# Decoding float64 weights in a routed-expert kernel: the weights' low halves made on VectorE, and the mantissa tail merged with the sign

## The chip, the cores and the metric

The kernel runs on one core of a Trainium2 chip. The metric is the device time of one launch in microseconds (us), the median of several runs. A profiled execution of the same program gives the trace; its own time is given beside its span below.

The engines are named as in the profile: PE (TensorE, the matrix multiplier), DVE (VectorE), ACT (ScalarE), POOL (GpSimd) and SP (which issues most of the loads).

## The reference

Three stages, one after the other, on 2304 tokens (4 batches of 576) of width 512:

```python
# 1. masked attention, 8 heads of 64; heads 0-3 see a local band of 32, heads 4-7 every 32nd position
scores = q @ k.T / 8;  attn = softmax(where(mask, scores, -1e9));  x = attn @ v
# 2. MLP with a PReLU, 512 -> 2048 -> 512, weights given as float64
h = x @ w_in;  g = maximum(h, 0) + alpha * minimum(h, 0);  x = g @ w_out
# 3. one of 8 experts for each token (argmax of x @ w_gate), 512 -> 1024 -> 512
y[t] = gate[t] * sigmoid(...)[t] * (relu(x[t] @ w1[e]) @ w2[e])
```

Only stage 1 and the first sixth of stage 2 matter here: that is where the float64 weights are turned into a form that PE can multiply.

## The kernel before

**The work and its order.** The MLP is cut into 6 blocks of 384 tokens and 16 chunks of 128 hidden columns; `n` counts the 96 pairs of block and chunk. For each `n`, `mlp_in` makes a 128x384 tile of h with 12 matmuls (lines 439 to 441), `mlp_act` applies the PReLU (ACT, lines 448 and 449; DVE, line 450), `mlp_split` splits the result into a high part `gh` (ACT, line 459) and a low part `gl` (DVE, line 460), and `mlp_out` adds it to three accumulators with 9 matmuls (lines 473 to 475). Three products of high and low parts stand in for one fp32 product. The loop runs two ahead: iteration `n` multiplies the weights of `n + 2` into h and the result of `n` into the accumulators.

Attention is cut into 48 steps. The first ten and their tails fill a prologue of 13 steps (about 6 to 47 us); the others are spread over the MLP loop, one in nearly each iteration of block 0. A step has its scores (PE), their maximum (DVE, line 252), the exponentials (ACT, line 281), the sums' reciprocals (DVE, lines 295 and 296), the normalisation (POOL, line 297), transposes (PE, line 313; ACT, line 315), the product with the values (PE, line 328) and its split into `xh` (ACT, line 367) and `xl` (DVE, line 372). The order on every engine is the order in which the code is written; each engine works its own list from the top.

**The decoding of a chunk.** A chunk's weights come as 128x1024 float64, loaded by SP into `raw` (in the code `raw64`), 8 KB for each partition. Each float64 is two 32-bit words, the low one first. Five instructions and a sixth turn them into fp32 and then into a high and a low part:

- `decode_a` (line 402, ACT): the upper word, read as a float and scaled, into a `stage` tile;
- `decode_b` (line 406, DVE): the stage tile shifted left by 3, which makes room for 3 more bits; (line 407, DVE): the low word shifted right by 29, ORed into it;
- `decode_s` (line 413, DVE): the sign of the upper word, ORed into it;
- `decode_c` (line 421, ACT): the high half of `w`, a rounded copy; (line 422, POOL): the low half, the difference.

The 16 chunks are decoded once, in the prologue (chunks 0 to 4) and in the first iterations of block 0 (5 to 15), and all 6 blocks use them. In iteration `n` the loop issues `decode_c` of chunk `n + 4`, `decode_b` and `decode_s` of chunk `n + 5`, and `decode_a` of chunk `n + 6`. `stage` has three buffers. The main loop, cut to what matters:

```python
if n + 2 < last: mlp_in(n + 2)
...                                     # values of an attention step
if n + 2 < last: mlp_act(n + 2)
if n + DEC < NC1: decode(n + DEC, 4)
...                                     # scores and maximum of a step
if n + DEC + 1 < NC1: decode(n + DEC + 1, 3)
mlp_out(n, range(1))                    # transposes, then the rest of mlp_out
if n + DEC + 2 < NC1: decode(n + DEC + 2, 1)
if n + 2 < last: mlp_split(n + 2)
```

Here `DEC` is 4, `NC1` is 16, and `decode(k, m)` issues those of the first `m` decoding steps of chunk `k` that were not issued before.

Of the kernel before, what the change touches and what calls it, by code (L numbers as in the profile page):

```python
# [7 lines left out]
F32 = mybir.dt.float32  # L8
F32R = mybir.dt.float32r
BF16 = mybir.dt.bfloat16  # L10
I32 = mybir.dt.int32
AF = mybir.ActivationFunctionType
ALU = mybir.AluOpType
X = mybir.AxisListType.X
# [9 lines left out]
NC1 = FF // P  # L24
# [18 lines left out]
DEC = 4  # L43
# [19 lines left out]
RS = 7  # L63
NEG = -1.0e9
BIG = 12582912.0
SIGN = -(2**31)

C_ID = 0
C_I8 = C_ID + P
# [14 lines left out]
def attention_prelu_mlp_routed_experts_kernel(  # L84
# [11 lines left out]
    nc = tc.nc  # L96
# [28 lines left out]
    with tc.manual_schedule():  # L125
# [144 lines left out]
        def att_exp(gi):  # L270
# [6 lines left out]
            if b < PE_MASK:  # L277
                nc.scalar.activation(out=nm[:r, : 2 * nj], in_=nm[:r, : 2 * nj], func=AF.Copy, scale=SCALE)
            for u in range(2 * nj):
# [3 lines left out]
                    in_=src,  # L283
                    func=AF.Exp,
                    bias=nm[:r, u : u + 1],
# [18 lines left out]
        def att_transpose(gi, tag):  # L304
# [9 lines left out]
            ptt = apool.tile([P, 4, P], F32, tag="pt", name="ptt", bufs=NPT_BUFS)  # L314
            nc.scalar.activation(out=ptt[:kk, :nu, :r], in_=tr[:kk, :nu, :r], func=AF.Copy)
            pt_t[gi] = ptt
# [20 lines left out]
        def att_store(gi):  # L337
# [28 lines left out]
            for src, dh, dl in moves:  # L366
                nc.scalar.activation(out=dh, in_=src, func=AF.Copy)
            px_t[gi] = moves
# [8 lines left out]
        raw_t, w_t = {}, {}  # L377

        def stage():
            return xpool.tile([P, 2 * (DM + 1)], F32, tag="stage", name="stage", bufs=3)  # L380
# [8 lines left out]
        def load_w(c):  # L389
            raw_t[c] = w_tile(c, I32, "raw64")  # L390
            nc.sync.dma_start(raw_t[c], wp[c].bitcast(I32))


        dec_t = {}

        def words(c):
            two = raw_t[c].rearrange("p (n two) -> p n two", two=2)
            return two[:, :, 0], two[:, :, 1]

        def decode_a(c):  # L400
            t = dec_t[c] = stage()[:, :1024]
            nc.scalar.activation(out=t, in_=words(c)[1].bitcast(F32), func=AF.Copy, scale=2.0**-112)

        def decode_b(c):
            t = dec_t[c].bitcast(I32)
            nc.vector.tensor_scalar(out=t, in0=t, scalar1=3, scalar2=None, op0=ALU.logical_shift_left)
            nc.vector.scalar_tensor_tensor(
                out=t, in0=words(c)[0], scalar=29, in1=t, op0=ALU.logical_shift_right, op1=ALU.bitwise_or
            )

        def decode_s(c):
            t = dec_t[c].bitcast(I32)
            nc.vector.scalar_tensor_tensor(
                out=t, in0=words(c)[1], scalar=SIGN, in1=t, op0=ALU.bitwise_and, op1=ALU.bitwise_or
            )
            raw_t.pop(c)

        def decode_c(c):
            t = dec_t.pop(c)
            w = w_t[c] = w_tile(c, F32R, "w")  # L420
            nc.scalar.activation(out=w[:, :1024], in_=t, func=AF.Copy)
            nc.gpsimd.tensor_tensor(out=w[:, 1024:], in0=t, in1=w[:, :1024].bitcast(F32), op=ALU.subtract)

        def w_in(c, part, k):
            return w_t[c][:, part * 1024 + k * P : part * 1024 + (k + 1) * P]
# [29 lines left out]
        def mlp_split(n):  # L455
            v = h_t.pop(n)
            gh = xpool.tile([P, BLK], F32R, tag="gh", name="gh", bufs=3)
            gl = xpool.tile([P, BLK], F32R, tag="gl", name="gl", bufs=2)
            nc.scalar.activation(out=gh, in_=v, func=AF.Copy)  # L459
            nc.vector.tensor_tensor(out=gl, in0=v, in1=gh.bitcast(F32), op=ALU.subtract)  # L460
            g_t[n] = (gh, gl)
# [606 lines left out]
        def load_ws(k):  # L1068
            for _, c in zip(range(k), loads):
                load_w(c)  # L1070
# [49 lines left out]
        steps_done = {}  # L1120

        def decode(k, n):

            steps = [decode_a, decode_b, decode_s, decode_c]
            for f in steps[steps_done.get(k, 0) : n]:
                f(k)
            steps_done[k] = max(steps_done.get(k, 0), min(n, 4))

        for s in range(NPRO):
            att_step(s, ("h", "h") if s % 2 else ("S", "X"), "acc0" if s % 2 else "T", "acc1" if s % 2 else "acc2")  # L1130
# [4 lines left out]
            if s == 4:  # L1135
# [3 lines left out]
                    out=wg_hl[:, :, 2 * E :], in0=wg_sb, in1=wg_hl[:, :, : 2 * E].bitcast(F32), op=ALU.subtract  # L1139
                )  # L1140
                nc.vector.memset(acc_oh[:, 0, :], 0.0)
            for k in range(NC1):
                n = s - (T0[k] if k < len(T0) else 99)
                if n >= 0:
                    decode(k, n + 1)

        span[:] = [FIRST + EXTRA if EXTRA < LV else 0, NG]
        decode(DEC, 3)
        decode(DEC + 1, 1)
        for n in range(2):  # L1150
            mlp_in(n, range(KD - 1, KD))
            mlp_act(n)
            mlp_split(n)
        last = NBLK * NC1
        turn_at, logits_at = {}, {}
        for blk in range(NBLK - 1):
            for j in range(TPB):
                c = 2 * j + 1 if blk < NBLK - 2 else j
# [11 lines left out]
        for n in range(last):  # L1170
            blk, c = divmod(n, NC1)
            todo = []
            if blk + 1 < len(steps_of) and c < NC1 - 2:
                s0, s1 = steps_of[blk + 1]
                k = s1 - s0
# [38 lines left out]
                rank(blk - 1)  # L1214
            mlp_out(n, range(2, TPB))
            load_ws(1)
            if n + DEC + 2 < NC1:
                decode(n + DEC + 2, 1)
            if n + 2 < last:
                mlp_split(n + 2)  # L1220
            if c == NC1 - 1 and blk == 3:
                s_a.close()
                epool = s_x.enter_context(tc.tile_pool(name="epool", bufs=1))
                idx_in = epool.tile([P, NSLOT], I32, name="idx_in")
                idx_out = epool.tile([P, NSLOT], I32, name="idx_out")
                idx_any = epool.tile([1, 1], I32, name="idx_any")
# [265 lines left out]
```

## Time and profile before

| what | value |
|---|---|
| median of 3 runs | 828.43 us (828.38 to 828.44) |
| the profiled execution | 827.54 us |
| its span, first to last instruction | 825.8 us |
| PE busy | 783.3 us (95% of the span) |
| DVE busy | 465.1 us (56%) |
| ACT busy | 427.6 us (52%) |
| POOL busy | 223.9 us (27%) |
| mean granted clock of PE | 0.978 |

The profiled execution is 0.89 us under the median and 1.74 us over its own span. A granted clock of 1.00 is 2.4 GHz, and 0.50 would be 1.2 GHz throughout.

How rows read. A timeline row has its start in us from the span's start, its length in us, the engine, the line of the code, the operation, output<-inputs, shapes, a count, and in brackets the idle time before it with what ended that. A row of a table of windows has the stretch, its length, the busy us of PE, PE's weight loads, DVE, ACT and POOL (with counts of instructions), the granted clock of PE, the share of the DMA engines and GB/s. A row of a group has its count, busy us, mean ns, and the idle time before it. A row of one line has minimum, median and maximum in ns.

### The profile page before, as it was taken

What the parts mean: (1) busy time and instruction counts of PE and PEld (TensorE: products, weight loads), DVE (VectorE), ACT (ScalarE), POOL (GpSimd) and SP (SyncE); (2) the same over time, 40 slices, a digit from 0 to 9 for tenths busy, and PEclk for the clock granted to TensorE, in tenths of its full rate; (3) what the DMA queues carried; (4) which work ended last, traced back from release to release, by engine and by line L of the source; (5) the groups of instructions that cost most, each with busy time, mean ns of one, the idle gap of its engine ahead of it and who ended that gap; (6) DMA issues with size and microseconds to landing.
All of it is one profiled execution on the core that took longest, in us unless ns stands there. A gap on an engine that the chain in (4) does not pass through costs nothing. (4 is left out here: it accounts for less than half of the span.)

```text
span 825.8 us, 13693 instructions
## 1 busy us (share of the span) xinstructions
PE 783.3 (95%) x5035; PEld 659.0 (80%) x5035; DVE 465.1 (56%) x980; ACT 427.6 (52%) x1057; POOL 223.9 (27%) x152
## 2 busy tenths in 40 slices
PE   7778889999999999999999999999989998999996
PEld 4566767888888888888898898889879876878884
DVE  4979997345544454556333434657695447854422
ACT  6847676445544454555333333265534656655542
POOL 2734444011100011111000000113474465546422
PEclk9789899999999999999999999999999999999998
DMA  9707411111200121101000100553224577787421
GB/s 342 303 1 298 167 56 49 33 33 46 84 18 1 47 87 64 36 11 39 2 1 1 39 1 1 204 191 125 56 90 159 176 268 250 281 290 270 161 88 41
DMA packets 22621, 91.04 MB, mean 110 GB/s; under 512 B 3082, under 2 KB 7312, under 8 KB 15376
## 3 DMA queue, kind: packets, MB, share of 16 engines
q1 hardware_dynamic: 18816, 78.52, 26.8%
q0 software_dynamic: 3728, 11.55, 4.0%
q8 instruction: 41, 0.67, 0.3%
q14 instruction: 36, 0.29, 0.1%
HBM read 105.78 MB, written 9.97 MB: 140 GB/s over the span
## 5 line engine op out<-in xcount | busy, mean ns | idle before, releaser
L439 PE MATMUL h<-xh,w 128*128 128x384 f32 x384 | 131.2, 342 | 4.1 <-DVE gl L460 3.8
L440 PE MATMUL h<-xl,w 128*128 128x384 f32 x384 | 130.5, 340 | 0.7 <-DVE xl L372 0.7
L441 PE MATMUL h<-xh,w 128*128 128x384 f32 x384 | 130.4, 340 | 0.0
L450 DVE SCALAR_TENSOR_TENSOR h<-h,nalpha,a 128x384 f32<-128x384 f32 x96 | 59.9, 624 | 116.1 <-ACT h L449 116.0
L473 PE MATMUL acc<-w,gh 128*128 128x512 f32 x288 | 125.3, 435 | 0.0
L297 POOL TENSOR_TENSOR p<-p,sm 96x512 f32<-96x512 f32 (+2 forms) x47 | 48.2, 1026 | 283.6 <-DVE sm L296 260.5
L888 DVE TENSOR_TENSOR wx<-raw,wx 128x1024 fp32r<-128x1024 f32 x72 | 97.1, 1392 | 46.9 <-ACT wx L886 46.6
L475 PE MATMUL acc<-w,gl 128*128 128x512 f32 x288 | 114.3, 397 | 0.0
L474 PE MATMUL acc<-w,gh 128*128 128x512 f32 x288 | 114.1, 396 | 0.0
L448 ACT ACTIVATE a<-h 128x384 f32<-128x384 f32 x96 | 47.2, 491 | 105.9 <-PE h L441 105.9
L886 ACT ACTIVATE wx<-raw 128x1024 fp32r<-128x1024 f32 x96 | 94.6, 1056 | 7.6 <-DMA raw<-in_wexp_dram 7.6
L1042 PE MATMUL acc<-wx,hh 128*128 128x512 f32 x304 | 97.0, 401 | 0.0
L888 POOL TENSOR_TENSOR wx<-raw,wx 128x1024 fp32r<-128x1024 f32 x24 | 63.1, 2629 | 90.7 <-ACT wx L886 90.6
L439 PEld LDWEIGHTS h<-xh,w 128*128 128x128 f32 x384 | 73.4, 191 | 9.6 <-DVE gl L460 5.5
L440 PEld LDWEIGHTS h<-xl,w 128*128 128x128 f32 x384 | 73.2, 191 | 4.8 <-DVE xl L372 1.0
L441 PEld LDWEIGHTS h<-xh,w 128*128 128x128 f32 x384 | 73.2, 191 | 0.0
L460 DVE TENSOR_TENSOR gl<-h,gh 128x384 fp32r<-128x384 f32 x96 | 53.3, 555 | 33.0 <-PE acc L475 18.2
L895 POOL DMA_INDIRECT xg<-rows,idx_in x23 | 29.3, 1274 | 145.4 <-ACT h L449 139.0
L1042 PEld LDWEIGHTS acc<-wx,hh 128*128 128x128 f32 x304 | 56.6, 191 | 11.2
L475 PEld LDWEIGHTS acc<-w,gl 128*128 128x128 f32 x288 | 54.6, 190 | 13.2
L459 ACT ACTIVATE gh<-h 128x384 fp32r<-128x384 f32 x96 | 46.7, 486 | 34.8 <-DVE h L450 34.7
L473 PEld LDWEIGHTS acc<-w,gh 128*128 128x128 f32 x288 | 54.5, 189 | 10.6 <-issue 0.3
(259 smaller groups left out, 1548.3 us busy)
## 6 DMA issues: line engine op xcount, KB each, us to landing
raw<-in_wexp_dram SPq DMA_DIRECT2D x64, 1024.0 KB
raw<-in_wp_dram SPq DMA_DIRECT2D x16, 1024.0 KB
qk<-in_qkv_dram SPq DMA_DIRECT2D x10, 576.0 KB
rows<-stage SPq DMA_DIRECT2D x15, 256.5 KB
v<-in_qkv_dram SPq DMA_DIRECT2D x8, 320.0 KB
qk<-in_qkv_dram SPq DMA_DIRECT2D x4, 384.0 KB
v<-in_qkv_dram SPq DMA_DIRECT2D x6, 256.0 KB
qk<-in_qkv_dram SPq DMA_DIRECT2D x4, 224.0 KB
```

Source lines behind the costliest of these rows:

```text
L297: (nc.vector if gi in NRV else nc.gpsimd).tensor_tensor(out=pt[:r, :nu, :kk], in0=pt[:r, :nu, :kk], in1=sm[:r, :nu].unsqueeze(2).to_broadc ...
L439: mm(ph[:, :BLK], w_in(c, 0, k), xh[:, k, :], start=(k == 0), stop=False)
L440: mm(ph[:, :BLK], w_in(c, 0, k), xl[:, k, :], start=False, stop=False)
L441: mm(ph[:, :BLK], w_in(c, 1, k), xh[:, k, :], start=False, stop=(k == KD - 1))
L450: nc.vector.scalar_tensor_tensor(out=v, in0=v, scalar=nalpha[:, c : c + 1], in1=a, op0=ALU.mult, op1=ALU.add)
L460: nc.vector.tensor_tensor(out=gl, in0=v, in1=gh.bitcast(F32), op=ALU.subtract)
L473: mm(o, gh[:, t], w_out(c, 0), start=(c == 0), stop=False)
L474: mm(o, gh[:, t], w_out(c, 1), start=False, stop=False)
L475: mm(o, gl[:, t], w_out(c, 0), start=False, stop=(c == NC1 - 1))
L886: nc.scalar.activation(out=w[:, :1024], in_=raw, func=AF.Copy)
L888: eng.tensor_tensor(out=w[:, 1024:], in0=raw, in1=w[:, :1024].bitcast(F32), op=ALU.subtract)
L1042: mm(po[i], h[:, h0 : h0 + P], wk[:, w0 : w0 + 512], start=st, stop=sp)
```

## The change

Two things are altered in the decoding. First, the 3 bits that the low word gives (its top 3) are no longer ORed in by an instruction of their own. A shift on 16-bit quarters (line 410 of the changed code) takes quarter 1 of each float64, shifts it right by 13 and writes it over quarter 2, the lower half of the upper word, in `raw` itself; `decode_a` has read that word before. The masked step of line 417 then takes the sign bit and those 3 bits out of the upper word together. Second, the low half of `w` is made by DVE (line 428) and not by POOL, in a step of its own, `decode_d`, which is issued later: behind `mlp_out` in the loop, one attention step later in the prologue. `decode(DEC + 1, 1)` moves from ahead of the first two `mlp_act` to behind them.

```diff
-SIGN = -(2**31)
+SIGN_AND_TAIL = -(2**31) + 7
...
         def decode_b(c):
             t = dec_t[c].bitcast(I32)
+            q = raw_t[c].bitcast(U16).rearrange("p (n four) -> p n four", four=4)
+            nc.vector.tensor_scalar(
+                out=q[:, :, 2], in0=q[:, :, 1], scalar1=13, scalar2=None, op0=ALU.logical_shift_right
+            )
             nc.vector.tensor_scalar(out=t, in0=t, scalar1=3, scalar2=None, op0=ALU.logical_shift_left)
-            nc.vector.scalar_tensor_tensor(
-                out=t, in0=words(c)[0], scalar=29, in1=t, op0=ALU.logical_shift_right, op1=ALU.bitwise_or
-            )
 
         def decode_s(c):
...
             nc.vector.scalar_tensor_tensor(
-                out=t, in0=words(c)[1], scalar=SIGN, in1=t, op0=ALU.bitwise_and, op1=ALU.bitwise_or
+                out=t, in0=words(c)[1], scalar=SIGN_AND_TAIL, in1=t, op0=ALU.bitwise_and, op1=ALU.bitwise_or
             )
...
         def decode_c(c):
-            t = dec_t.pop(c)
             w = w_t[c] = w_tile(c, F32R, "w")
-            nc.scalar.activation(out=w[:, :1024], in_=t, func=AF.Copy)
-            nc.gpsimd.tensor_tensor(out=w[:, 1024:], in0=t, in1=w[:, :1024].bitcast(F32), op=ALU.subtract)
+            nc.scalar.activation(out=w[:, :1024], in_=dec_t[c], func=AF.Copy)
+
+        def decode_d(c):
+            w = w_t[c]
+            nc.vector.tensor_tensor(
+                out=w[:, 1024:], in0=dec_t.pop(c), in1=w[:, :1024].bitcast(F32), op=ALU.subtract
+            )
...
-            steps = [decode_a, decode_b, decode_s, decode_c]
+            steps = [decode_a, decode_b, decode_s, decode_c, decode_d]
...
-        decode(DEC, 3)
-        decode(DEC + 1, 1)
         for n in range(2):
             mlp_in(n, range(KD - 1, KD))
             mlp_act(n)
             mlp_split(n)
+        decode(DEC, 3)
+        decode(DEC + 1, 1)
...
             mlp_out(n, range(2, TPB))
             load_ws(1)
+            if n + DEC < NC1:
+                decode(n + DEC, 5)
             if n + DEC + 2 < NC1:
                 decode(n + DEC + 2, 1)
```

DVE in one iteration of the loop (`n` = 1), before; the numbered `raw` is chunk 6:

```order
L450 SCALAR_TENSOR_TENSOR h<-h,nalpha,a 128x384
L252 TENSOR_REDUCE nm<-sl_bank 126x2
L252 TENSOR_REDUCE nm<-X 126x2
L406 TENSOR_SCALAR stage<-stage 128x1024
L407 SCALAR_TENSOR_TENSOR stage<-raw_533,stage 128x1024
L413 SCALAR_TENSOR_TENSOR stage<-raw_533,stage 128x1024
L460 TENSOR_TENSOR gl<-h,gh 128x384
```

and with the change:

```order
L458 SCALAR_TENSOR_TENSOR h<-h,nalpha,a 128x384
L253 TENSOR_REDUCE nm<-sl_bank 126x2
L253 TENSOR_REDUCE nm<-X 126x2
L410 TENSOR_SCALAR raw_532<-raw_532 128x1024
L413 TENSOR_SCALAR stage<-stage 128x1024
L417 SCALAR_TENSOR_TENSOR stage<-raw_532,stage 128x1024
L428 TENSOR_TENSOR w<-stage,w 128x1024
L468 TENSOR_TENSOR gl<-h,gh 128x384
```

The two-input step of line 407 is gone; the shift of quarters stands ahead of the other shift, and the subtraction for chunk 5 stands ahead of `gl`.

POOL in the same part of the loop, before:

```order
L297 TENSOR_TENSOR p<-p,sm 96x512
L422 TENSOR_TENSOR w<-stage,w 128x1024
L297 TENSOR_TENSOR p<-p,sm 126x4x126
L422 TENSOR_TENSOR w<-stage,w 128x1024
L297 TENSOR_TENSOR p<-p,sm 126x4x126
L422 TENSOR_TENSOR w<-stage,w 128x1024
```

and with the change:

```order
L298 TENSOR_TENSOR p<-p,sm 96x512
L298 TENSOR_TENSOR p<-p,sm 126x4x126 x2
L298 TENSOR_TENSOR p<-p,sm 72x2x72
L298 TENSOR_TENSOR p<-p,sm 96x512
L298 TENSOR_TENSOR p<-p,sm 126x4x126 x2
```

Only the normalisations are left on POOL in this stretch.

## Rows read from the trace of the kernel before

**Rows 1.** Table of windows: the prologue, the loop's parts, all that follows block 0.

```profile
14.30:49.30 35.00, 25.97 (x184) 16.99 (x180) 33.04 (x61) 25.85 (x91) 22.93 (x11) 0.85 0.64 254
49.30:62.53 13.23, 11.45 (x51) 10.25 (x52) 8.52 (x11) 6.22 (x12) 2.49 (x1) 0.75 0.05 13
62.53:136.59 74.06, 62.87 (x382) 49.03 (x380) 71.74 (x105) 52.60 (x154) 33.43 (x19) 0.95 0.42 151
136.59:148.69 12.10, 11.87 (x84) 9.79 (x85) 5.05 (x15) 7.32 (x29) 5.47 (x4) 1.00 0.13 38
154.15:590.00 435.85, 435.01 (x2676) 377.44 (x2675) 211.09 (x579) 201.01 (x568) 44.84 (x40) 1.00 0.15 51
```

**Rows 2.** Table of waits, DVE's own, 62.53 to 136.59: total us, times, longest.

```profile
DVE xl L372 <- ACT xh L367: 1.0, 1, 1.0
DVE h L450 <- ACT h L449: 0.3, 1, 0.3
```

**Rows 3.** Timeline of DVE, one iteration of the loop.

```profile
100.04 0.15 DVE L295 TENSOR_SCALAR sm<-sm 96x4 f32<-96x4 f32 x1
...
101.56 0.41 DVE L252 TENSOR_REDUCE nm<-X 126x2 f32<-126x252 f32 x1
101.88 2.65 DVE L406 TENSOR_SCALAR stage<-stage 128x1024 int32<-128x1024 int32 x1
104.57 1.22 DVE L407 SCALAR_TENSOR_TENSOR stage<-raw,stage 128x1024 int32<-128x1024 int32 x1
105.83 1.22 DVE L413 SCALAR_TENSOR_TENSOR stage<-raw,stage 128x1024 int32<-128x1024 int32 x1
```

**Rows 4.** Timeline of POOL in the same iteration.

```profile
100.57 1.04 POOL L297 TENSOR_TENSOR p<-p,sm 96x512 f32<-96x512 f32 x1 [3.98 <-DVE sm L296]
101.57 2.42 POOL L422 TENSOR_TENSOR w<-stage,w 128x1024 fp32r<-128x1024 f32 x1
```

**Rows 5.** Groups of DVE instructions, 62.53 to 136.59.

```profile
L406 DVE TENSOR_SCALAR stage<-stage 128x1024 int32<-128x1024 int32 x10 | 21.1, 2106 | 0.0
L407 DVE SCALAR_TENSOR_TENSOR stage<-raw,stage 128x1024 int32<-128x1024 int32 x10 | 18.4, 1845 | 0.3
```

**Rows 6.** Single lines over the whole span: minimum, median and maximum in ns.

```profile
L406 DVE TENSOR_SCALAR stage<-stage x16: 675/804/2997, 14.3 to 130.6; 128x1024 int32<-128x1024 int32 x16
...
L888 DVE TENSOR_TENSOR wx<-raw,wx x72: 1210/1220/3426, 543.8 to 807.6; 128x1024 fp32r<-128x1024 f32 x72
...
L422 POOL TENSOR_TENSOR w<-stage,w x16: 2355/2498/3350, 23.0 to 137.6; 128x1024 fp32r<-128x1024 f32 x16
```

**Rows 7.** Timeline of DVE: the PReLU step that marks an iteration.

```profile
62.53 0.62 DVE L450 SCALAR_TENSOR_TENSOR h<-h,nalpha,a 128x384 f32<-128x384 f32 x1
...
136.59 0.62 DVE L450 SCALAR_TENSOR_TENSOR h<-h,nalpha,a 128x384 f32<-128x384 f32 x1
...
148.69 0.62 DVE L450 SCALAR_TENSOR_TENSOR h<-h,nalpha,a 128x384 f32<-128x384 f32 x1 [0.41 <-ACT h L449]
```

**Rows 8.** Timeline of DVE, prologue and the loop's first iteration.

```profile
24.28 2.05 DVE L295 TENSOR_SCALAR sm<-sm 126x4 f32<-126x4 f32 x1
...
32.87 0.81 DVE L295 TENSOR_SCALAR sm<-sm 126x4 f32<-126x4 f32 x1 [0.78 <-ACT p L281]
...
39.43 2.33 DVE L295 TENSOR_SCALAR sm<-sm 72x2 f32<-72x2 f32 x1
...
46.20 3.18 DVE L413 SCALAR_TENSOR_TENSOR stage<-raw,stage 128x1024 int32<-128x1024 int32 x1
49.30 0.61 DVE L450 SCALAR_TENSOR_TENSOR h<-h,nalpha,a 128x384 f32<-128x384 f32 x1
...
57.55 3.34 DVE L407 SCALAR_TENSOR_TENSOR stage<-raw,stage 128x1024 int32<-128x1024 int32 x1
```

**Rows 9.** Timelines of ACT and PE around the end of the prologue.

```profile
47.30 0.49 ACT L449 ACTIVATE h<-h 128x384 f32<-128x384 f32 x1
...
51.08 0.69 PE L439 MATMUL h<-xh,w 128*128 128x384 f32 x1 [3.69 <-DVE gl L460]
```

More of the change, by code (lines that the diff above doesn't have):

```diff
@@ L11 @@
 I32 = mybir.dt.int32
+U16 = mybir.dt.uint16
 AF = mybir.ActivationFunctionType
@@ L1122, in decode @@
         def decode(k, n):
-            steps = [decode_a, decode_b, decode_s, decode_c]
+            steps = [decode_a, decode_b, decode_s, decode_c, decode_d]
             for f in steps[steps_done.get(k, 0) : n]:
                 f(k)
-            steps_done[k] = max(steps_done.get(k, 0), min(n, 4))
+            steps_done[k] = max(steps_done.get(k, 0), min(n, 5))
         for s in range(NPRO):
```

## Prediction, made before the changed kernel ran

> **What bounds the kernel now.** I read the table of windows first. From 154.15 us on PE is busy 435.01 of 435.85 us while DVE has half of its time free [rows 1]: whatever comes before that only moves the rest forward or back, us for us. Before it the order is the other way round. In the ten loop iterations from 62.53 to 136.59 us DVE is busy 71.74 of 74.06 us and PE only 62.87, at a granted clock of 0.95 (1.00 is 2.4 GHz); in the prologue, 14.30 to 49.30 us, DVE is busy 33.04 of 35.00 us, PE 25.97 [rows 1]. In those ten iterations DVE's own waits come to 1.3 us together [rows 2], so the others wait for DVE. An iteration takes (136.59 - 62.53) / 10 = 7.41 us; the two behind them, with attention but with no decoding left on DVE, take 12.10 / 2 = 6.05 us, and there PE is full and at 1.00 [rows 1, 7]. So 6.05 us is what PE needs, and DVE costs 1.36 us more in each iteration.
>
> The timeline of one iteration says why. Line 406 takes 2.65 us there, and the 128x1024 steps behind it 1.22 us each [rows 3]; line 406 alone takes 0.68 us [rows 6]. While it is stuck, POOL makes a low half, 101.57 to 103.99 us [rows 4], and line 406 ends 0.54 us after that. In the next case it is line 407 that is stuck, for 3.34 us [rows 8]. One of the two is held in every iteration: over the ten their means are 2.11 and 1.85 us instead of 0.68 and 1.22 [rows 5], which is (2.11 - 0.68) + (1.85 - 1.22) = 2.06 us of an iteration. POOL's subtraction costs DVE about what one on DVE would cost, and more.
>
> **The change, part by part.**
>
> *A, the ten iterations.* Removed from DVE: the 2.06 us of being held, and line 407 itself, 1.22 us [rows 3]. Added: the subtraction and the shift of quarters. The subtraction has a row of its own kind, 128x1024 fp32r from two fp32 tiles: 1.21 us undisturbed [rows 6]. The shift is not in the trace: 1024 two-byte elements, 8 bytes apart, in and out. From below it is bounded by line 406, also a one-input shift of 1024 elements, 0.68 us [rows 6]; I see no reason for less, since the elements are not dense. From above it is bounded by line 407, which reads one input 8 bytes apart at 1.22 us and is no slower than line 413 or the dense subtraction [rows 3, 6], so the step in itself costs a reader nothing. I take 0.68 us, the row of the same operation. One more instruction adds one gap, 0.04 us (104.57 - 101.88 - 2.65) [rows 3]. DVE's iteration becomes 7.41 - 2.06 - 1.22 + 0.68 + 1.21 + 0.04 = 6.06 us. PE's need is 6.05 us. Two engines that are equally full and wait for each other do not both run without gaps; I take 6.2 us. Gain: 74.06 - 62.0 = 12.1 us.
>
> The Trainium skill, VectorE: DVE Perf Modes, in "What auto-detection actually checks", lets an instruction with one source and both sides in SBUF run two results a cycle, and asks for a step of one element only for packing two-byte values. By that rule the shift costs what line 406 does; were it to fall to one result a cycle, the row of line 407 would be its price and the time would be that of the first rival below.
>
> *B, the iteration before them* (from 56.30 to 62.53 us, without attention). Line 407 is held there, 3.34 us [rows 8]. The change removes 3.34 and adds 0.68 + 1.21 + 0.04: 1.4 us less on DVE. The clock in that window is 0.75 [rows 1], so PE is near; I take 1.0 us.
>
> *C, the prologue.* POOL's four subtractions hold three tiny steps (line 295: 2.05, 0.81 and 2.33 us, where 0.15 is normal [rows 3]) and the last masked step (3.18 instead of 1.22 us) [rows 8]: 1.90 + 0.66 + 2.18 + 1.96 = 6.7 us. Five steps of line 407 become shifts, 5 x 0.54 = 2.7 us less. Four subtractions come in, 4 x 1.21 = 4.8 us more. Sum 4.6 us less on an engine that is busy 94% of that stretch [rows 1]. That is the upper end, because ACT and PE have chains of their own there. The lower end is the last hold alone: ACT ends line 449 at 47.79 us, and line 450 starts only at 49.30 [rows 8, 9], 1.5 us later, and PE then waits 3.69 us for the `gl` behind it [rows 9]. I take the middle, 3.0 us.
>
> *What moves at no cost.* `decode_a` of chunk 5 (ACT, 1.1 us) goes behind the first two PReLUs; PE's wait of 3.69 us [rows 9] covers it, and without that cover it would delay the third `gh` by its length once. The low half is now ready some 3 us later than POOL had it, but its chunk is multiplied two iterations on. The subtraction adds a wait of DVE for ACT's high half; ACT starts that right behind line 449, as DVE starts line 450, and five DVE steps lie between. Queued behind it on DVE is `gl`, for which PE waits. `raw` stays in use exactly as long as before, so SP's loads and every DMA keep their place. The `stage` buffer is freed one part of an iteration later, and ACT writes it again an iteration after that.
>
> *Sum.* 12.1 + 1.0 + 3.0 = 16.1 us off the profiled 827.54: 811.4 us. The median stands 0.89 us above that execution, so **812.3 us**.
>
> **The rivals.**
>
> *The shift runs at half the pace*, 1.22 us. For it: its elements are two bytes wide and apart, unlike line 406's. Against: line 406 is otherwise the same operation. DVE's iteration is then 6.60 us, with the same addition of 0.14 about 6.75; A gives 6.6, B 0.9 and C 2.0 us (5 x 0.54 = 2.7 us less on DVE there): 9.5 us, **818.9 us**.
>
> *POOL still holds DVE.* The normalisations stay on POOL (1.04 us), one in each iteration. Now they run from 100.57 to 101.61 us, while DVE does steps that are not held, and the first shift comes at 101.88 [rows 3, 4]: 0.27 us later. If that margin went, the shift would be held by up to 1.04 us in each of the ten iterations: 10.4 us of A are lost, **822.7 us**. Against: the five DVE steps between the reciprocal and the shift are the same ones, in the same order. The Trainium skill, SBUF — State Buffer, "Who interferes with whom", has DVE's two-input steps contend with any GpSimd instruction that reads SBUF, and one-input steps in a two-port mode shut it out and be shut out. That speaks against putting both new steps on DVE while POOL keeps a task; no run here shows it for a 2-byte shift.
>
> *Slower: the shift writes badly.* Every output is two bytes in the middle of a word and 8 bytes from the next; no row shows such a write. If it takes what POOL's pass over as many elements takes, 2.50 us [rows 6], DVE's iteration is 6.06 + 1.82 = 7.88 us: A loses 4.7 us, B 0.4 and C 4.5 (5 x 1.82 less 4.6), together 9.6 us, **838.0 us**. It decides against the change in the loop from a shift of 0.68 + 1.35 = 2.03 us. For it: nothing but the gap in the trace. Against: strided reads cost nothing here.
>
> *It does not do what it says:* the holds are not POOL's. Then the 2.06 us stay, and the iteration is 7.41 - 1.22 + 0.68 + 1.25 = 8.1 us, 7 us slower. Against: each of the holds in the loop ends within about a step's length of POOL's subtraction. This is the same side as the last one and counts with it.
>
> **How the numbers follow.** The forecast, a shift near 0.68 us and no new hold, has 0.66; the shift at half pace 0.17; POOL's normalisation holding DVE 0.07; the two slower ones 0.07 together; 0.03 for a gain that ACT or PE eat up wholly. About 0.2% (1.7 us) is what a measurement here can tell from no change. Low end: A at PE's 6.05 us gives 13.6, B 1.4, C 4.6, and the clock something besides: at 0.75 over 13.23 us [rows 1] about 3.3 us of full-speed work are lost, and half of that may come back if PE waits less, 1.7 us. Sum 21.3, so 807 us. High end: the half-pace rival with C at 1.5 and B at 0.5, 8.6 us, so 820 us. The range 807 to 820 leaves out POOL's hold and the slower cases. Faster 0.91, same 0.03, slower 0.06.
>
> **What would show it.** Right: the ten iterations measured from PReLU step to PReLU step at 6.1 to 6.3 us; line 413 of the changed code (the old shift) at 0.68 us and line 417 at 1.22 us with hardly any spread; the shift of quarters at about 0.68; the subtraction at 1.21; PE's granted clock up in 49 to 137 us; everything after block 0 as long as before. Wrong: a shift at 1.2 us or above; spread in lines 410, 413 or 428 that ends with a normalisation on POOL; DVE waiting for ACT ahead of line 428; or the loop at 6.2 us and the end not earlier, which would mean that time is given back behind 154 us.

## The result, and the profile after

The changed kernel takes **814.92 us** (median of four runs, 814.50 to 817.12), the kernel before 828.43 us beside it (four runs, 828.38 to 831.42): 13.5 us less, a ratio of 0.9834 with a 95% interval of 0.9805 to 0.9862. The forecast was 812.3 us, its range 807 to 820. The execution that was profiled is the longest of the four, 817.12 us; against the profiled 827.54 us of before it is 10.4 us shorter, and what separates 10.4 from 13.5 comes up below.

Lines of the changed kernel have moved: the reciprocal is line 297 and POOL's normalisation 298 (296 and 297 before), the shift of quarters is line 410, the old shift 413 (406), the masked step 417 (413), the subtraction, now on DVE, 428 (422), the PReLU step 458 (450). Line 407 is gone.

The profile's first part, of the changed kernel: span, then busy time, share and instructions of each engine.

```profile
span 815.3 us, 13671 instructions
...
PE 780.9 (96%) x5032; PEld 658.7 (81%) x5035; DVE 453.8 (56%) x996; ACT 427.6 (52%) x1057; POOL 182.8 (22%) x136
```

DVE has 16 instructions more and POOL 16 fewer, which are the subtractions. The table of windows follows, cut at the same PReLU steps as [rows 1]: prologue, the steps before the ten iterations, the ten iterations, the two behind them, and a long stretch of what follows block 0.

```profile
15.22:48.76 33.54, 25.00 (x182) 16.51 (x180) 31.36 (x66) 24.91 (x90) 12.12 (x7) 0.85 0.63 250
48.76:60.59 11.83, 10.05 (x48) 9.08 (x49) 7.50 (x12) 7.91 (x14) 0.00 (x0) 0.86 0.01 0
60.59:123.49 62.90, 59.65 (x386) 47.84 (x384) 62.21 (x115) 51.80 (x153) 8.09 (x9) 1.00 0.48 176
123.49:135.58 12.09, 11.86 (x84) 9.80 (x85) 6.10 (x16) 7.20 (x29) 3.11 (x3) 1.00 0.20 64
141.08:536.97 395.89, 395.05 (x2376) 339.80 (x2375) 186.75 (x531) 180.54 (x537) 30.73 (x31) 1.00 0.13 44
```

Ten iterations take 62.90 us instead of 74.06 [rows 1], 6.29 us each instead of 7.41. DVE is still the engine that is full in them: busy 62.21 of 62.90 us, and the table of its own waits is empty there, where it had 1.3 us [rows 2]. POOL's 33.43 busy us have shrunk to 8.09, the normalisations alone. PE's granted clock is 1.00 instead of 0.95. The last window ends with the last PReLU step; before, the stretch between the same two places took 395.88 us, so behind block 0 nothing was given back up to there.

The timeline of DVE, one iteration of the changed kernel, beside [rows 3]:

```profile
98.10 0.61 DVE L458 SCALAR_TENSOR_TENSOR h<-h,nalpha,a 128x384 f32<-128x384 f32 x1
98.62 0.41 DVE L253 TENSOR_REDUCE nm<-sl_bank 126x2 f32<-126x252 f32 x1
98.95 0.41 DVE L253 TENSOR_REDUCE nm<-X 126x2 f32<-126x252 f32 x1
99.28 1.36 DVE L410 TENSOR_SCALAR raw<-raw 128x1024 uint16<-128x1024 uint16 x1
100.41 0.76 DVE L413 TENSOR_SCALAR stage<-stage 128x1024 int32<-128x1024 int32 x1
101.20 1.23 DVE L417 SCALAR_TENSOR_TENSOR stage<-raw,stage 128x1024 int32<-128x1024 int32 x1
102.34 1.22 DVE L428 TENSOR_TENSOR w<-stage,w 128x1024 fp32r<-128x1024 f32 x1
103.47 0.55 DVE L468 TENSOR_TENSOR gl<-h,gh 128x384 fp32r<-128x384 f32 x1
```

and of POOL in it, beside [rows 4]:

```profile
98.15 1.03 POOL L298 TENSOR_TENSOR p<-p,sm 126x504 f32<-126x504 f32 x1 [5.45 <-DVE sm L297]
```

Three things stand here. The old shift, line 413, takes 0.76 us; it took 2.65 us in [rows 3]. POOL's normalisation ends at 99.18 us, 0.10 us ahead of the first long step of this iteration. And the shift of quarters takes 1.36 us, not 0.68. The groups of DVE's long steps in the ten iterations say the same of all of them, beside [rows 5]:

```profile
L410 DVE TENSOR_SCALAR raw<-raw 128x1024 uint16<-128x1024 uint16 x10 | 13.6, 1361 | 0.0
L417 DVE SCALAR_TENSOR_TENSOR stage<-raw,stage 128x1024 int32<-128x1024 int32 x10 | 12.3, 1225 | 0.3
L428 DVE TENSOR_TENSOR w<-stage,w 128x1024 fp32r<-128x1024 f32 x10 | 12.2, 1218 | 0.0
L413 DVE TENSOR_SCALAR stage<-stage 128x1024 int32<-128x1024 int32 x10 | 7.3, 731 | 0.0
```

The 0.10 us are not there in every iteration. In four of the ten the normalisation ends 0.12 to 0.24 us behind the start of the shift. In the two where that is most, the shift takes 1.44 and 1.45 us instead of 1.32 to 1.36. One of them, DVE's line and POOL's:

```profile
105.28 1.45 DVE L410 TENSOR_SCALAR raw<-raw 128x1024 uint16<-128x1024 uint16 x1
```

```profile
104.48 1.03 POOL L298 TENSOR_TENSOR p<-p,sm 126x504 f32<-126x504 f32 x1 [5.30 <-DVE sm L297]
```

**Where the time went.** Stretches between marks of the timelines, in us. The marks are DVE's first instruction of line 295 (296 now) and PReLU steps by number; the last column runs from the last PReLU step to the end of the span. "Changed again" is the same kernel in experiment 10 (below).

| | start to first mark | to 1st PReLU | to 4th | to 14th (ten iterations) | to 96th, the last | to the end |
|---|---|---|---|---|---|---|
| before | 8.40 | 40.90 | 13.23 | 74.06 | 413.44 | 275.77 |
| changed | 9.32 | 39.44 | 11.83 | 62.90 | 413.48 | 278.33 |
| changed again | 8.54 | 39.20 | 11.78 | 62.89 | 413.42 | 276.87 |

In the profiled execution the gain is 1.46 us in the prologue, 1.40 in the next stretch and 11.16 in the ten iterations. Of these 14.0 us, 0.92 are lost ahead of the first mark and 2.56 behind the last PReLU step, in the expert stage, where the instructions are the same. In experiment 10's execution of the same kernel those two losses are 0.14 and 1.10 us; in a third one, experiment 1, they are 0.91 and 2.51 us, near the first. So the second to fourth columns are the change; what stands ahead of them and behind block 0 differs between executions of one kernel.

### The profile page after: what moved, and what is told of

The parts are those of the page before. It is cut to its first block, busy times and chain, and to the rows that moved or that the text cites. A ratio compares the mean times of both kernels' runs of the same rounds, so it can differ in the third digit from the quotient of the medians.

```text
span 815.3 us, 13671 instructions
## 1 busy us (share of the span) xinstructions
PE 780.9 (96%) x5032; PEld 658.7 (81%) x5035; DVE 453.8 (56%) x996; ACT 427.6 (52%) x1057; POOL 182.8 (22%) x136
## 4 chain that ended last, share of the span: by engine, by line
PE 75%; DVE 9%; issue 3%; ACT 3%; POOL 0%; DMA 0%; SPq 0%; ACTq 0%; DVEq 0%; POOLq 0%
PE acc L1050 10%; PE acc L481 8%; PE acc L483 7%; PE h L447 7%; PE h L449 7%; PE acc L482 7%; PE h L448 7%; PE T L329 2%; PE sl_bank L235 2%; DVE wx L896 2%; PE T L314 1%; PE h L973 1%; PE h L975 1%; PE h L974 1%; PE sl_bank L914 1%
## 5 line engine op out<-in xcount | busy, mean ns | idle before, releaser
L298 POOL TENSOR_TENSOR p<-p,sm 96x512 f32<-96x512 f32 (+2 forms) x47 | 49.9, 1061 | 331.0 <-DVE sm L297 278.0
```

The source lines that it names most:

```text
L298: (nc.vector if gi in NRV else nc.gpsimd).tensor_tensor(out=pt[:r, :nu, :kk], in0=pt[:r, :nu, :kk], in1=sm[:r, :nu].unsqueeze(2).to_broadc ...
```

## The experiments

Each difference is against the changed kernel. On the three chips the kernel before had medians of 829.22 us (first four runs), 827.98 (next four) and 828.23 (last three); ratios are against the one on the same chip.

**1. The changed kernel as it is** (r1_same). No edit.

> The changed kernel again, unaltered. In its first profile the lead over the kernel before is 13.07 us from the end of block 0 to the end of the MLP, and 10.5 us at the end: 2.6 us are lost in the expert stage. Theory A (chance of that one execution, in the loads of the experts' weights): the new profile keeps a lead of about 13 us to its end, time 814.5 to 815.1 us. Theory B (the change itself costs time behind the MLP): the new profile loses 2 to 3 us in the expert stage again, time about 817 us. Ten loop iterations about 62.9 us by either.

Measured: 816.93 us (four runs), ratio 0.9853 (0.9820 to 0.9885); ten iterations 62.89 us; from the last PReLU step to the end 278.28 us. The loop repeats to 0.01 us, and the longer expert stage came back too, which by this run alone looked like a property of the new schedule. Experiments 2, 6 and 10 say more on that.

**2. The subtraction back on POOL** (r2_pool_sub), the merged shift kept.

```diff
         def decode_c(c):
...
+            nc.gpsimd.tensor_tensor(out=w[:, 1024:], in0=dec_t.pop(c), in1=w[:, :1024].bitcast(F32), op=ALU.subtract)
         def decode_d(c):
-            w = w_t[c]
-            nc.vector.tensor_tensor(
...
+            pass
```

> The changed kernel with one part undone: the subtraction of the low half is on POOL again, right behind ACT's high half; the shift of quarters and the merged mask stay. Theory A (the holds of DVE by POOL's subtraction are what the change removed, so that they come back): about 2 us of holding in each of ten iterations, iteration 7.2 to 7.4 us, the kernel at 826 to 828 us. Theory B (the new shift, one input and one result a cycle, is not held, so that POOL's pass runs beside it and only the rest of the pass holds the step behind): holding about 1 us, iteration 6.2 to 6.5 us, the kernel at 815 to 818 us, and the subtraction could have stayed on POOL.

Measured: 827.14 us (12 runs), ratio 0.9982 (0.9963 to 1.0000): nearly the whole gain is gone. The ten iterations take 73.14 us, 7.31 each. The groups of DVE's instructions in them:

```profile
L410 DVE TENSOR_SCALAR raw<-raw 128x1024 uint16<-128x1024 uint16 x10 | 23.2, 2321 | 0.0
...
L413 DVE TENSOR_SCALAR stage<-stage 128x1024 int32<-128x1024 int32 x10 | 15.7, 1570 | 0.0
L417 DVE SCALAR_TENSOR_TENSOR stage<-raw,stage 128x1024 int32<-128x1024 int32 x10 | 14.3, 1430 | 0.3
```

One iteration of the same kernel, DVE's timeline, and POOL's:

```profile
101.32 3.29 DVE L410 TENSOR_SCALAR raw<-raw 128x1024 uint16<-128x1024 uint16 x1
```

```profile
101.00 2.42 POOL L425 TENSOR_TENSOR w<-stage,w 128x1024 fp32r<-128x1024 f32 x1
```

The loop's long holds are back with POOL's subtraction: against the changed kernel the means of the three steps are up by 0.96, 0.84 and 0.20 us, 2.0 us of an iteration. POOL's step ends at 103.42 us and the shift 1.19 us later, somewhat less than its own length behind it. The 2-byte shift is held like the 4-byte one, though it runs at half the pace of that (experiments 5 and 9).

**3. The old way to put the quarter in** (r3_old_tail), the subtraction left on DVE.

```diff
-SIGN_AND_TAIL = -(2**31) + 7
+SIGN_AND_TAIL = -(2**31)
...
-            q = raw_t[c].bitcast(U16).rearrange("p (n four) -> p n four", four=4)
-            nc.vector.tensor_scalar(
-                out=q[:, :, 2], in0=q[:, :, 1], scalar1=13, scalar2=None, op0=ALU.logical_shift_right
-            )
...
+            nc.vector.scalar_tensor_tensor(
+                out=t, in0=words(c)[0], scalar=29, in1=t, op0=ALU.logical_shift_right, op1=ALU.bitwise_or
+            )
```

> The changed kernel with the other part undone: the low word is shifted and ORed in by a two-input step again, as before, and there is no shift of quarters; the subtraction stays on DVE. Theory A (removing POOL's pass from beside DVE is the main gain): no holds, iteration 2.31 + 0.71 + 1.26 + 1.15 + 1.14 = 6.6 us at most, the kernel at 816 to 819 us. Theory B (the gain came with the shift): iteration 7.2 us or more, the kernel at 825 us or above.

Measured: 817.17 us (four runs), ratio 0.9847 (0.9815 to 0.9878); ten iterations 63.72 us, 6.37 each. The groups:

```profile
L410 DVE SCALAR_TENSOR_TENSOR stage<-raw,stage 128x1024 int32<-128x1024 int32 x10 | 12.2, 1225 | 0.3
L416 DVE SCALAR_TENSOR_TENSOR stage<-raw,stage 128x1024 int32<-128x1024 int32 x10 | 12.2, 1224 | 0.3
L427 DVE TENSOR_TENSOR w<-stage,w 128x1024 fp32r<-128x1024 f32 x10 | 12.2, 1218 | 0.0
L409 DVE TENSOR_SCALAR stage<-stage 128x1024 int32<-128x1024 int32 x10 | 7.0, 700 | 0.0
```

So the whole gain of the loop but 0.8 us is the subtraction's move. The second half of the change, the merged step, is worth 63.72 - 62.90 = 0.8 us in the ten iterations, and in the medians nothing that these runs tell apart. The two halves add to within 0.2 us: in the profiled executions the last PReLU step comes at 550.03 us before, at 549.05 with the merged step alone (experiment 2), at 537.79 with the move alone and at 536.97 with both.

**4. No quarter at all** (r4_no_tail): as experiment 3, without the old step that is added there; the 3 lowest bits are left out.

> The changed kernel without the shift of quarters: the lowest 3 bits of the mantissa are left out and the mask takes the sign alone. DVE has 1.1 us less in each iteration. Theory A (DVE still sets the pace at 6.29 us): the iteration falls to what PE needs, 6.05 us or a little above, the kernel 2 to 3 us faster than the changed one, about 812.5 us. Theory B (PE and its waits already set 6.29 us): iteration 6.2 to 6.3 us, the kernel within 1 us of the changed one.

Measured: 811.75 us (five runs), ratio 0.9786 (0.9759 to 0.9813); ten iterations 60.33 us, 6.03 each. The window of them, and DVE's own waits there:

```profile
57.26:117.59 60.33, 59.31 (x387) 48.70 (x387) 52.26 (x104) 51.33 (x154) 8.53 (x10) 1.00 0.49 180
```

```profile
DVE h L454 <- ACT h L453: 2.9, 9, 0.5
DVE xl L373 <- ACT xh L368: 2.7, 6, 0.6
DVE sm L296 <- ACT p L282: 1.2, 2, 0.9
```

Now PE is full, 59.31 of 60.33 us, DVE has 8 us free and waits for ACT. That is the floor under the loop, 6.03 us an iteration. It also prices the shift: 0.26 us per iteration of the loop lies over that floor, half of the 5.2 us between the medians of experiments 1 and 4; 1.4 us more are gained in the prologue and 0.9 in the stretch behind it.

**5. What makes the shift slow** (r5_prices). The shift's line takes another form from chunk to chunk: another element size, another distance.

```diff
+            v = (0, 1, 2, 3, 0, 4, 1, 2, 3, 0, 4, 1, 2, 3, 0, 4)[c]
+            if v == 0:
                 ...
+            elif v == 1:
+                nc.vector.tensor_scalar(out=r32[:, :, 0], in0=r32[:, :, 0], scalar1=29, ...)
+            elif v == 2:
+                nc.vector.tensor_scalar(out=r16[:, :1024], in0=r16[:, :1024], scalar1=0, ...)
+            elif v == 3:
+                nc.vector.tensor_scalar(out=t2[:, :, 0], in0=t2[:, :, 0], scalar1=0, ...)
+            else:
+                nc.vector.tensor_scalar(out=r8[:, :, 4], in0=r8[:, :, 3], scalar1=5, ...)
```

> The changed kernel with the shift in five forms, one form for each chunk, 1024 elements each, done in place; the 3 bits are left out in all of them and the mask takes the sign alone. Forms: 2-byte elements 8 bytes apart (as in the change); 4-byte elements 8 bytes apart; 2-byte elements side by side; 2-byte elements 4 bytes apart; single bytes 8 bytes apart. Read where POOL is idle. Theory A (the 8-byte step costs the pace): 4-byte elements 8 bytes apart take 1.2 to 1.3 us as well, 2-byte elements 4 bytes apart about 0.7 us. Theory B (2-byte elements that are not side by side cost it): 4-byte elements 8 bytes apart take 0.7 us, 2-byte elements 4 bytes apart 1.2 to 1.3 us. By both, 2-byte elements side by side take 0.4 to 0.7 us.

Measured, in DVE's timeline of the loop: line 415 is the form of the change, 419 whole 4-byte words that lie 8 bytes apart, 423 2-byte elements side by side, 428 2-byte elements 4 bytes apart, 432 single bytes 8 bytes apart. Each has 128x1024 elements.

```profile
76.88 1.34 DVE L415 TENSOR_SCALAR raw<-raw 128x1024 uint16<-128x1024 uint16 x1
...
83.38 1.33 DVE L432 TENSOR_SCALAR raw<-raw 128x1024 uint8<-128x1024 uint8 x1
...
89.86 0.69 DVE L419 TENSOR_SCALAR raw<-raw 128x1024 int32<-128x1024 int32 x1
...
95.59 0.41 DVE L423 TENSOR_SCALAR raw<-raw 128x1024 uint16<-128x1024 uint16 x1
...
101.22 0.77 DVE L428 TENSOR_SCALAR raw<-raw 128x1024 uint16<-128x1024 uint16 x1
```

Neither theory of this run fits. The distance of 8 bytes is not it (0.69 us with words), and 2-byte elements apart are not it either (0.77 us at 4 bytes). Among these forms only elements smaller than a word and 8 bytes apart fall to 1.33 us. That is what was seen, and not yet the rule: the forms that keep the pace lie one or two elements apart, the slow ones four or eight, so a rule by the step in elements fits as well. Words 16 bytes apart would tell the two from each other; they were not run.

**6. The kernel before once more** (r6_before_again).

> The kernel before, unaltered, profiled again. The stretch from the last PReLU step of the MLP to the end was 275.7 us in its first profile and 277.7 to 278.3 us in the five profiles since, the one with the subtraction back on POOL among them. Theory A (the length of that stretch differs by execution or chip): about 278 us here, time about 829 us. Theory B (the kernels with the changed decoding lose it): 275.7 us again.

Measured: 828.01 us; from the last PReLU step to the end 275.78 us, as in the first profile of it (275.77). The expert stage of this kernel was short twice.

**7. POOL's normalisations of the prologue on DVE** (r7_norm_dve).

```diff
-NRV = (9,)
+NRV = tuple(range(10))
```

> The changed kernel with the nine normalisations of the prologue moved from POOL to DVE (the tenth is on DVE already). In the changed kernel POOL's normalisations hold DVE five times there, 3.7 us in all, and are themselves held to 2.1 us. Theory A (these holds are where the prologue's gain went): each normalisation costs DVE about 0.6 us, 5 us in all, but the holds of 3.7 us and the waits of PE for POOL go: the first PReLU step 0.5 to 2 us earlier, kernel 0.5 to 2 us faster than the changed one on the same chip (816.9). Theory B (DVE's own work sets the prologue): first PReLU step 1 to 2 us later, kernel 1 to 2 us slower.

Measured: 814.80 us (five runs), ratio 0.9840 (0.9822 to 0.9858). First mark to first PReLU step: 37.57 us instead of 39.44. The holds it removes are these, in the changed kernel's DVE timeline of the prologue, where lines 413 and 417 or 428 take 0.70 and 1.21 us when nothing holds them:

```profile
16.33 1.56 DVE L413 TENSOR_SCALAR stage<-stage 128x1024 int32<-128x1024 int32 x1
...
23.12 1.54 DVE L413 TENSOR_SCALAR stage<-stage 128x1024 int32<-128x1024 int32 x1
...
26.87 2.05 DVE L417 SCALAR_TENSOR_TENSOR stage<-raw,stage 128x1024 int32<-128x1024 int32 x1
...
33.78 1.55 DVE L428 TENSOR_TENSOR w<-stage,w 128x1024 fp32r<-128x1024 f32 x1
...
38.24 1.55 DVE L413 TENSOR_SCALAR stage<-stage 128x1024 int32<-128x1024 int32 x1
```

They come to 3.7 us. POOL's normalisation ahead of the third of them starts together with DVE's subtraction (line 428, 25.73 to 26.95 us) and is 2.09 us long; the one at 33.22 us, beside DVE's short steps, takes 1.03 us:

```profile
25.74 2.09 POOL L298 TENSOR_TENSOR p<-p,sm 126x504 f32<-126x504 f32 x1 [1.63 <-DVE sm L297]
```

So POOL holds DVE and is held by it in the same place. On DVE the normalisation takes 0.68 us and nothing is held. In this execution the gain at the first PReLU step is 1.9 us; experiment 11 shows less of it.

**8. The subtraction one part of the iteration earlier** (r8_sub_early).

```diff
-                decode(n + DEC, 4)
+                decode(n + DEC, 5)
```

> The changed kernel with the subtraction issued where the high half is, right behind the PReLU step, and not behind the masked step, in the loop alone. Theory A (its place hides DVE's wait for ACT's high half): ACT starts the high half as DVE starts line 458, and takes 1.06 us; DVE then waits about 0.6 us in each of ten iterations, iteration 6.9 us, kernel 5 to 6 us slower than the changed one (816.9). Theory B (the place is of no matter, since DVE waits elsewhere for less): iteration 6.3 us, kernel within 1 us.

Measured: 818.47 us (four runs), ratio 0.9876 (0.9856 to 0.9895); ten iterations 67.62 us, 6.76 each. Two iterations' subtractions in DVE's timeline:

```profile
89.18 1.23 DVE L428 TENSOR_TENSOR w<-stage,w 128x1024 fp32r<-128x1024 f32 x1 [0.34 <-ACT w L424]
...
95.67 1.46 DVE L428 TENSOR_TENSOR w<-stage,w 128x1024 fp32r<-128x1024 f32 x1
```

The one waits for ACT's high half; the other is held by POOL's normalisation, which starts at 95.02 us there. In the ten iterations the holds of the subtraction come to 2.9 us, in seven of them, while DVE's waits for ACT are 1.5 us, of which only 0.34 us is for the high half. So theory A was near on the iteration (6.9 us), but the wait that it named is the small part, and POOL the large one; and the kernel is 1.5 us over the 816.9 it named, on another chip than that, not 5 to 6. Where the subtraction stands is worth 0.47 us in each iteration; the change put it at a place where neither happens.

**9. The shift's price, all forms 8 bytes apart** (r9_prices2).

```diff
+            o, i, s = (
+                (q[:, :, 2], q[:, :, 1], 13),
+                (q[:, :, 1], q[:, :, 1], 13),
+                (r32[:, :, 0], r32[:, :, 1], 29),
+                (q[:, :, 0], q[:, :, 1], 13),
+                (r8[:, :, 3], r8[:, :, 3], 5),
+            )[c % 5]
+            nc.vector.tensor_scalar(out=o, in0=i, scalar1=s, scalar2=None, op0=ALU.logical_shift_right)
```

> As the run with five forms, with five others; the 3 bits are left out and the mask takes the sign alone. In the first set the two slow forms (1.3 us) were also the only two that wrote into another 32-bit word than they read. Forms now, 8 bytes apart all: quarter 1 into quarter 2 (as in the change); quarter 1 in place; upper word into lower word, 4 bytes each; quarter 1 into quarter 0 of the same word; byte 3 in place. Theory A (elements narrower than a word and 8 bytes apart cost the pace): the three 2-byte forms and the byte form take 1.2 to 1.35 us, the 4-byte form 0.7 us. Theory B (reading one word and writing another costs it): quarter 1 into 2 and upper into lower word take 1.2 to 1.35 us, the three others 0.7 us.

Measured, in DVE's timeline: a quarter shifted in its own place (chunk 6), a whole word to the word beside it (7), a quarter to the lowest one (8), a byte in its own place (9).

```profile
61.30 1.33 DVE L419 TENSOR_SCALAR raw<-raw 128x1024 uint16<-128x1024 uint16 x1
...
67.38 0.68 DVE L419 TENSOR_SCALAR raw<-raw 128x1024 int32<-128x1024 int32 x1
...
72.89 1.31 DVE L419 TENSOR_SCALAR raw<-raw 128x1024 uint16<-128x1024 uint16 x1
...
80.52 1.35 DVE L419 TENSOR_SCALAR raw<-raw 128x1024 uint8<-128x1024 uint8 x1
```

It does not matter whether the element moves, nor where to. A whole word at this distance takes 0.68 us, a part of one twice as long. These forms too leave open whether the distance in bytes or the step in elements decides.

**10 and 11. The changed kernel and experiment 7 again, on one chip** (r10_same2, r11_norm_dve2).

> The changed kernel once more, to stand beside the next run on one chip. Lead at the end of the MLP 13.1 us; between 814.5 and 817 us, by what the clock of PE does in the first 7 us and behind the router's small matmuls.

> The changed kernel with the prologue's normalisations on DVE, beside the changed kernel on one chip. Theory A (the 1.9 us of its first profile are real and reach the end): 1 to 3 us faster than the changed one. Theory B (they are given back by PE's clock or lie within what executions differ by): within 0.7 us.

Measured: the changed kernel 814.98 us (five runs, ratio 0.9853, 0.9826 to 0.9880), with the normalisations on DVE 813.61 us (five runs, 0.9838, 0.9808 to 0.9868). The medians are 1.4 us apart and the intervals overlap, so whether this version beats the changed kernel is not settled. The 1.9 us of experiment 7 did not come back: from the first mark to the first PReLU step the two took 39.20 and 38.96 us. The holds are gone in this execution too, but DVE waits 3.6 us for ACT's exponentials up to that step, and 2.1 us in experiment 7. So the 1.4 us are in theory A's range without what theory A gave as their reason. By its medians it is the best of the versions that compute everything. The expert stage took 276.87 and 276.09 us in these two.

**What the end of the program shows.** The window of 8 us right behind the 24 small matmuls of the router, in the changed kernel and in the one before; the third number from the end is PE's granted clock.

```profile
556.97:564.97 8.00, 8.00 (x57) 8.00 (x58) 4.13 (x21) 1.41 (x4) 3.21 (x5) 0.79 0.72 270
```

```profile
570.03:578.03 8.00, 8.00 (x70) 8.00 (x71) 4.33 (x21) 1.41 (x4) 3.20 (x5) 1.00 0.72 271
```

PE is full in both; at 0.79 it gets through 57 matmuls in place of 70, which is 8.00 x (1 - 57/70) = 1.5 us. In narrower windows of the changed kernel the granted clock is 1.00 up to 559.30 us, 0.50 (1.2 GHz) from 560.30 to 562.30, and 1.00 again from 563.30; PE is busy throughout. The clock is low at this place in experiments 1, 4, 9 and 10 too, and 1.00 in 2, 3, 5, 6, 7, 8 and 11. Each kernel that was profiled more than once had the same there each time (the changed one three times low, the one before and experiment 7's twice each at 1.00), so it seems to go with the program; but experiments 3 and 4, neither of them with the merged step, differ, and which property of a program decides it isn't shown. It isn't the whole of the longer stage either: experiments 2, 3 and 7 take 278.05, 277.91 and 277.88 us there with the clock at 1.00, and 11, the same kernel as 7, takes 276.09. That part differs between executions; where it arises was not followed.

## Why the prediction was right, and where its steps were off

The time and the range held, and so did the mechanism: 13.5 us between medians where 16.1 were forecast. One of the prediction's own signs of being wrong came true all the same, a shift at 1.2 us or above. Step by step:

**"POOL's subtraction costs DVE about what one on DVE would cost, and more": shown.** Experiment 2 brings the holds back with the subtraction alone and the iteration to 7.31 us; experiment 3 has no hold in the loop without it. The rival that the holds are not POOL's is out.

**The shift of quarters, taken at 0.68 us, was mis-sized: 1.36 us.** It stands even above the upper bound of 1.22 us that the prediction took from line 407. "I see no reason" was the weak place: line 406 has whole words and line 407 too, so no row of before bore on small elements far apart, and the bounds were those of another thing. The Trainium skill, VectorE: DVE Perf Modes, "What auto-detection actually checks", gave two results a cycle by its conditions; the runs agree for words 8 bytes apart (0.69 us) and 2-byte elements 4 bytes apart (0.77 us), and disagree for 2-byte elements 8 bytes apart (1.34 us). So the condition of the first rival came true, and its time, 818.9 us, did not.

**The reason is a second error the other way, in the same sum.** The prediction added durations and gaps. What an iteration pays is the distance from start to start, and these steps overlap: the shift of 1.36 us is followed by the next step 100.41 - 99.28 = 1.13 us after its start, the subtraction of 1.22 us after 1.13. Line 407, which left, had cost 105.83 - 104.57 = 1.26 us [rows 3]. By distances the sum is 7.41 - 2.06 - 1.26 + 1.13 + 1.13 = 6.35 us, 0.05 more for line 413 (0.73 us in the mean instead of 0.68), and 0.13 less for DVE's own 1.3 us of waits in ten iterations [rows 2], which are gone: 6.27, measured 6.29. That the forecast of 6.2 us is off by only 0.09 is luck: the shift's 0.68 us too many are met by 0.39 of overlap (1.36 + 1.21 + 0.04 - 1.22 by durations, 1.13 + 1.13 - 1.26 by distances) and 0.13 of waits that went, and by the 0.14 us that were added for another reason. Term A, 12.1 us forecast, is 11.16.

**PE's need of 6.05 us an iteration: right.** Experiment 4 runs at 6.03. The 0.14 us that the prediction added because two full engines would get in each other's way was not needed, because they are not equally full: DVE still sets the loop.

**B, 1.0 us: 1.05 in the iteration that was meant.** The 1.40 us of the table are of the whole stretch from the first to the fourth PReLU step. From the third to the fourth, which is B, the kernel before took 6.23 us (56.30 to 62.53) and the changed one takes 5.18 (55.41 to 60.59), at a granted clock of 1.00 in both, so these 1.05 us aren't the clock's; DVE is busy nearly throughout in both, 6.16 and 5.14 us:

```profile
56.30:62.53 6.23, 6.23 (x36) 5.22 (x36) 6.16 (x6) 3.56 (x6) 2.49 (x1) 1.00 0.11 27
```

```profile
55.41:60.59 5.18, 5.18 (x32) 4.38 (x32) 5.14 (x7) 4.21 (x7) 0.00 (x0) 1.00 0.01 1
```

The other 0.35 us come ahead of it, from the first PReLU step to the third, where the clock was 0.53 and is 0.74. "The clock in that window is 0.75 [rows 1], so PE is near" was therefore a misreading: 0.75 is the mean of a part at 0.53 and of B's own part at 1.00. By distances the DVE steps alone give 1.05 us: line 407's 3.37 us went, 1.14 each for the shift and the subtraction came, and line 413 takes 0.04 more than line 406. So the 1.0 taken was right by luck.

**C, 3.0 us: 1.46, the lower end.** The holds of the tiny steps and of the last masked step went as said. But the shift gains less over line 407 than the 0.54 us taken. From start to start lines 406 and 407, with nothing held, took 1.86 us together in the prologue (44.14 to 46.00 us); now the two shifts take 1.12 us (44.29 to 45.41) and 0.63 (31.41 to 32.04). That is 0.11 us, and five of them give 0.55 instead of 2.7. With 6.7 - 4 x 1.14 + 0.55 = 2.7 us the middle that was taken could still nearly have been reached. What the prediction left out are holds by POOL's normalisations: they were in the prologue before already, on steps it did not look at. These are from DVE's timeline of the kernel before; undisturbed each takes 1.22 us.

```profile
15.02 1.95 DVE L407 SCALAR_TENSOR_TENSOR stage<-raw,stage 128x1024 int32<-128x1024 int32 x1
...
22.15 1.93 DVE L407 SCALAR_TENSOR_TENSOR stage<-raw,stage 128x1024 int32<-128x1024 int32 x1
...
34.20 1.98 DVE L413 SCALAR_TENSOR_TENSOR stage<-raw,stage 128x1024 int32<-128x1024 int32 x1
...
37.58 1.93 DVE L407 SCALAR_TENSOR_TENSOR stage<-raw,stage 128x1024 int32<-128x1024 int32 x1
```

They come to 2.9 us. Now such holds are 3.7 us (experiment 7), 0.8 us more, which leaves some 1.9 us for C. DVE's waits for ACT in the prologue have grown from 1.5 to 1.8 us, 0.8 of it a new wait for `xh` ahead of line 373. That comes to 1.6 us, measured 1.46.

**"POOL still holds DVE" came true in the loop for some 0.2 us, not for 10.4.** The margin of 0.27 us is 0.10 in the iteration shown and gone in four of the ten; yet the shift is held in only two of them, by 0.1 us each. Experiment 8 shows how near that is: one place earlier, and the subtraction meets POOL in seven of ten iterations. What the Trainium skill, SBUF — State Buffer, "Who interferes with whom", says of two-input steps and GpSimd is thus seen here, in the prologue (2.05 us in place of 1.21) and in experiment 2 (line 417, 1.43 us in the mean in place of 1.22); in the changed kernel's loop the order of the steps keeps them apart.

**"What moves at no cost": right** for the place of the subtraction (0.47 us an iteration if it is moved, experiment 8) and for block 0's end to the last PReLU step (413.44 and 413.48 us).

**"Everything after block 0 as long as before": wrong by 1.1 to 2.6 us,** in the expert stage. It had no term in the sum. With what is lost ahead of the first mark (0.92 and 0.14 us) it explains why 14.0 us of gain in the three stretches became 10.5 us of span in the profiled execution, and 14.3 became 13.1 in experiment 10's (825.8 - 812.7). Part of it is PE's granted clock behind the router, part differs between executions, and neither is explained.

## What to carry to other kernels

When a DVE step shows two durations, one of them normal and the other ending a step's length after POOL's, count what POOL's instruction costs DVE, not what it costs POOL: here DVE did the work itself in 1.2 us and lost 2.06 us an iteration by having it done. Sum steps of a full engine from start to start in the timeline, not by their durations. Price a new access pattern only by a row with the same element size and the same distance; where there is none, that term's bounds are not bounds.

## What the runs showed of the hardware that was not expected

- A one-input shift of 128x1024 elements on DVE took 0.41 us with 2-byte elements side by side, 0.77 us with them 4 bytes apart, 1.31 to 1.37 us with them 8 bytes apart, 1.32 to 1.36 us with single bytes 8 bytes apart, and 0.68 us with 4-byte words 8 bytes apart (experiments 5 and 9, in the loop).
- The 2-byte form that runs at the slow pace is held by POOL all the same: 3.29 us beside a subtraction of POOL, in place of 1.34 (experiment 2).
- A step of 1.22 or 1.36 us lets the next one begin 1.13 us after its own start, where the next one doesn't read what it wrote (100.41 behind 99.28 us in the changed kernel). Where it does, line 413 behind line 407 before, 1.26 us lay between [rows 3].
- PE's granted clock was 0.79 over the 8 us behind 24 matmuls of 16 columns in the expert stage with some of the kernels and 1.00 with others, although their instructions there are the same.
